# Linear attention and a token/channel mixer: where the hand-over sums and the last products stand around the last batch

## The chip, the cores and the metric

The kernel runs on one core of a Trainium2 chip. The metric is device time in microseconds, lower is better. Engines are named as the profile names them: PE (TensorE matmul), PEld (its weight loads), DVE (VectorE), ACT (ScalarE), POOL (GpSimd), SP (SyncE, used for transfers).

## What is computed

Linear attention with elu+1 features over batch 8, 8 heads, 576 tokens, 64 columns a head; its output, with heads side by side (512 columns), goes through a mixer over tokens (576 to 256 and back) and one over channels (512 to 1536 and back), each with a residual sum.

```
def phi(x): return np.where(x > 0, x, np.exp(x) - 1.0) + 1.0
q_p, k_p = phi(q), phi(k)
kv  = einsum('bhsd,bhse->bhde', k_p, v);  z = k_p.sum(axis=2)
x   = einsum('bhsd,bhde->bhse', q_p, kv) / (einsum('bhsd,bhd->bhs', q_p, z) + 1e-6)
xt  = x.transpose(0, 2, 1)
u   = x + (relu(xt @ w_tok1) @ w_tok2).transpose(0, 2, 1)
out = u + relu(u @ w_ch1) @ w_ch2
```

## The kernel before

The batches run one after another. The 576 tokens of a batch are four full row tiles of 128 and a tail of 64; the tails of two batches share one tile. PE computes in bf16 into eight PSUM banks, each named by hand.

The channel mixer of a batch is `mm3` (u @ w_ch1, twelve slices `mc`, each evicted with relu by ACT or DVE into `cr`) and then its second product. For most batches the second product is in Strassen-Winograd form: seven half-size products (`pair_product`, L779, six matmuls each, for j = 0 and 1) instead of eight. `ORDER` is 1, 2, 6, 5, 7, 3, 4. Their operands need differences of blocks (`row_sums` on DVE, weight differences on DVE and POOL), and their results three PSUM tiles, X, Z and Y. `pair_end` (L788) adds u to a tile on DVE and, where a term is shared, a copy of it on POOL (L790). `pair_put` (L794) writes a batch out from POOL's queue.

For the batches 2 to 6 a loop builds a list `big` of PE's large steps (12 of `mm3`, then the 14 pair products) and a list `fill` of everything else, with the step that it follows: `put(b0 + 12, u_sums, which)` places an operation after big step 24. All engines take their instructions in the order in which this emits them. `b0` is 12 for batch 6, so steps b0 to b0 + 13 are its pair products. The next batch's attention and token mixer are among the fill, and its u reaches `uT` by DMA transposes (`utr_dma`, L512).

The last batch, 7, is emitted by `last_block` from a written string, `SEQUENCE`. Its letters are:

- `m` g i: `mix_first(g, i)`, product i of the *first* channel product, also in Winograd form, for slice group g (L703, four matmuls). It needs the weight differences of `first_sums` and the u differences of `u_sums` (L680, four DVE instructions that read `uT`). Results i = 1, 5 and 6 are copied by ACT (L712), 4 is evicted with relu by ACT (L710), 2, 3 and 7 are added to a held copy by DVE (L715) and pass a relu later (L686).
- `c` i: `mm3_tails(i)`, the tails of the last four batches (L557), relu by ACT (L559), in bank 2 or 3.
- `r` k: the four `row_sums` for two of six hidden slices (L653, DVE).
- `p` i j: `product(n, j, i)`, second channel product i for the row tile pair j (L733, six matmuls). Each is followed by a DVE sum into `obuf` (L739). Pair 0 is written out once, after p40 (L762); pair 1 in four parts, after p21, p71, p31 and p41 (L759). A half goes from SP's queue and a half from ACT's.
- `q` e third: `tail_third`, a third of the tails' second product (L579, four matmuls of 512 columns); after the last third a DVE sum (L583) and the output (L585).

A product that adds to a PSUM tile has to wait until the sum of the earlier product has read that tile: p60, p70 and p40 share one tile with p10, p30 follows p50, p20 stands alone; the same for pair 1. m02 and m12 both use bank 0. Batch 6's tile X lies in bank 2, tile Y in bank 3, tile Z in bank 0; c0 uses bank 2. Batch 1's `mm3` has its own list of banks, by mc.

Of the kernel before, what the change touches and what calls it, by code (L numbers as in the profile page):

```python
# [18 lines left out]
def kernel(  # L19
# [45 lines left out]
    def bank(at=None):  # L65
        if at is None:
            at, ring[1] = ring[1], (ring[1] + 1) % 4
        return psum[:, at]
# [453 lines left out]
    def mm3(n, mc, kjs=range(NDM), dve=False):  # L522
        b = n % 2
        if kjs[0] == 0:
            part_of[mc] = bank(None if n == 0 else (
                (0, 1, 0, 1, 2, 3, 0, 1, 2, 3, 0, 1) if n > 1 else
                (3, 5, 7, 0, 3, 1, 2, 0, 3, 1, 0, 1))[mc])
        ps = part_of[mc]
        for kj in kjs:
            nc.tensor.matmul(out=ps, lhsT=wc1[:, kj, 128 * mc:128 * mc + 128],  # L530
                             rhs=uTj[b][:, kj] if n < 2 else uT[b][:, :, kj],
                             start=(kj == 0), stop=(kj == NDM - 1))
        if kjs[-1] == NDM - 1 and dve:
            nc.vector.tensor_scalar(out=cr[b][:, mc, :], in0=ps, scalar1=0.0, scalar2=None,
                                    op0=ALU.max)
        elif kjs[-1] == NDM - 1:
            nc.scalar.activation(out=cr[b][:, mc, :], in_=ps, func=AF.Relu)  # L537
# [117 lines left out]
    def row_sums(n, which, k0, m):  # L655
        winograd(sb, [ablock(n, i, e) for e in range(2) for i in range(2)], which,
                 slice(k0, k0 + m))
# [10 lines left out]
    def cblock(m, h):  # L668
        return wc1[:, 2 * h:2 * h + 2, HM * m:HM * (m + 1)]

    def ublock(h, e):
        return uT[1][:, 2 * e:2 * e + 2, 2 * h:2 * h + 2]
# [11 lines left out]
    def mix_relu():  # L684
        o = mixed.pop(0)
        nc.vector.tensor_scalar(out=o, in0=o, scalar1=0.0, scalar2=None, op0=ALU.max)  # L686
# [6 lines left out]
    def mix_first(g, i):  # L693
        ps = bank({1: (1, 4, 7), 6: (1, 4, 7), 7: (1, 4, 7), 4: (1, 4, 7), 2: (0, 0, 0),
                   5: (5, 6, 5), 3: (5, 6, 5)}[i][g]).rearrange("p (j c) -> p j c", j=2)
        first = i in (1, 2, 5)
        lhs, rhs = {1: (cblock(0, 0), ublock(0, 0)), 2: (cblock(0, 1), ublock(1, 0)),
                    3: (sw[3], ublock(1, 1)), 4: (cblock(1, 1), tu[3]), 5: (sw[0], tu[0]),
                    6: (sw[1], tu[1]), 7: (sw[2], tu[2])}[i]
        for j in range(2):  # L700
            cs = slice(128 * (2 * g + j), 128 * (2 * g + j) + 128)
            for k_ in range(2):
                nc.tensor.matmul(out=ps[:, j], lhsT=lhs[:, k_, cs], rhs=rhs[:, :, k_],  # L703
                                 start=(first and j == 0 and k_ == 0), stop=(k_ == 1),
                                 skip_group_check=not first or j == 1)
        c1, c6, c5 = hold[g]
        held_back = len(mixed)
        dst = lambda m, e: cr[1][:, KH * m + 2 * g:KH * m + 2 * g + 2, HALF[e]]
        if i == 4:
            nc.scalar.activation(out=dst(1, 0), in_=ps, func=AF.Relu)  # L710
        elif i in (1, 6, 5):
            nc.scalar.copy(out={1: c1, 6: c6, 5: c5}[i], in_=ps)  # L712
        else:
            o, c = {2: (dst(0, 0), c1), 3: (dst(0, 1), c6), 7: (dst(1, 1), c5)}[i]
            nc.vector.tensor_tensor(out=o, in0=ps, in1=c, op=ALU.add)  # L715
            mixed.append(o)
        if held_back:
            mix_relu()
# [67 lines left out]
    def pair_end(n, tile_, d, c, i=None):  # L786
        o = live["o4"][:, d::2, HC[c]]
        nc.vector.tensor_tensor(out=o, in0=live[tile_], in1=u[n % 2][:, d::2, HC[c]], op=ALU.add)  # L788
        if i is not None:
            nc.gpsimd.tensor_tensor(out=o, in0=o, in1=part[i], op=ALU.add)  # L790

    def pair_put(n):
        for e in range(2):
            nc.gpsimd.dma_start(out=outv[n, :, e:e + 7:2], in_=live["o4"][half[e]])  # L794
# [2 lines left out]


    SEQUENCE = """m01 m02 m11 m05 m15 m06 m12 c0 m21 m03 m16 m07 c1 m25 m13 m22 m17 m04 c2 m26 m14
        m23 c3 m27 r0 c4 m24 r2 c5 q00 q01 p10 r4 p20 q02 p11 q10 p60  # L800
        p50 q11 p21 p70 q12 p30 p61 p40 p51 p71 p31 p41"""

    def last_block(n):
        for e in SEQUENCE.split():
            a = [int(c) for c in e[1:]]
            if e[0] == "m":
                mix_first(*a)
            elif e[0] == "c":
                mm3_tails(*a)
            elif e[0] == "p":  # L810
                product(n, a[1], a[0])
            elif e[0] == "q":
                tail_third(*a)
            else:
                while mixed:
                    mix_relu()
                for which in range(1, 5):
                    row_sums(n, which, a[0], 2)

    def m4s(n):  # L820
        return [lambda i=i, j=j: pair_product(n, i, j) for i in ORDER for j in range(2)]
# [117 lines left out]
    for mc in range(2):  # L939
        mm3(0, mc, range(0, 2))  # L940
# [88 lines left out]
    put = lambda s, fn, *a: fill.append((s, lambda: fn(*a)))  # L1029
# [53 lines left out]
    for n in range(2, B - 1):  # L1083
        p, b = divmod(n, 2)
        tail = int(n == 3)
        big = m3(n) + m3t * tail + m4s(n) + m4(p, [8]) * tail
        b0 = 12 + 3 * tail
        todo = dict(steps(n + 1))
        fill = []
        put = lambda s, fn, *a: fill.append((s, lambda: fn(*a)))  # L1090
        at = lambda s, *nms: [put(s, todo.pop(nm)) for nm in nms if nm in todo]

        def phi_at(nm, ex, ad, en):
            for g in range(2):
                if ex is not None:
                    put(ex[g], phi_exp, nm, n + 2, 2 * g, 2)
            for g in range(2):
                put(ad[g], phi_add, nm, n + 2, 2 * g, 2)
                put(en[g], phi_end, nm, n + 2, 2 * g, 2)

        at(1, "nd")
        if n + 2 < B:
            if n > 3:
                phi_at("k", None, (2, 2), (3, 4))
                put(5, load_all, n + 3, "k")
            if n != 3:
                phi_at("q", (7, 7), (8, 9), (9, 10))
            else:
                phi_at("k", (7, 7), (8, 9), (9, 10))
            put(10, *((qtr_dma, n + 2) if n != 3 else (load_all, n + 3, "k")))  # L1110
            if n == 2:
                for g in range(2):
                    put(10, phi_add, "k", n + 2, 2 * g, 2)
        at(7, "mm1")
        for s, k0 in ((11, 0), (12, 3)):
            for w in (1, 2):
                put(s, row_sums, n, w, k0, 3)
        if n == 3:
            phi_at("q", (12, 13), (13, 13), (14, 14))
            put(15, qtr_dma, n + 2)  # L1120
        at(13, "mm2a", "uta")
        put(14, row_sums, n, 3, 0, KH)
        put(b0 + 1, pair_copy, 0)
        if n == 2:
            for g in range(2):
                put(b0 + 1, phi_exp, "k", n + 2, 2 * g, 2)
                put(b0 + 2, phi_end, "k", n + 2, 2 * g, 2)
            put(b0 + 4, load_all, n + 3, "k")
        at(b0 + 3 - tail, "mm2b", "utb")
        put(b0 + 4 - tail, row_sums, n, 4, 0, KH)  # L1130
        put(b0 + 4 - tail, pair_end, n, "Z", 0, 0, 0)
        put(b0 + 5, pair_copy, 1)
        if n + 2 < B:
            for g in range(2):
                put(b0 + (5 if n == 2 else 2) + g, vcast, n + 2, g)
        put(b0 + 7, load_all, n + 3, "qv")
        put(b0 + 7, pair_copy, 2)
        if n > 2 and n + 3 < B:
            put(b0 + 8, k_exp, n + 3)
        put(b0 + 9, pair_end, n, "X", 1, 1, 2)  # L1140
        if n == B - 2:
            at(b0 + 6, "mm2t", "utt")
        at(b0 + 9, "mm2t")
        if n + 2 < B:
            put(b0 + 9, kv, n + 2, range(2))
        at(b0 + 9, "utt")
        put(b0 + 11, pair_end, n, "Y", 0, 1, 1)
        if n == B - 2:
            for which in range(1, 5):
                put(6, first_sums, which)  # L1150
                put(b0 + 12, u_sums, which)
        put(b0 + 13, pair_end, n, "X", 1, 0)
        put(b0 + 13, pair_put, n)
        assert not todo, todo
        run(big, sorted(fill, key=lambda e: e[0]))

# [30 lines left out]
```

## Time and profile before

| | |
|---|---|
| median of 6 runs | 251.55 us |
| the runs | 251.1, 251.88, 251.19, 253.54, 256.08, 251.21 us |
| profiled execution | 251.1 us, span 249.3 us |
| busy | PE 241.1, DVE 184.8, ACT 140.2, POOL 67.3 us |
| granted TensorE clock | 1.00 |

A profile gives one execution. Its span runs from the first to the last instruction; the time contains 1.8 us more around it. Times inside it are microseconds from the span's start. In a group's line the columns are line, engine, operation, what is written from what, count, busy time and mean; in a chain each row has start, length and what ran; in a timeline the same, with the engine's idle time before it in brackets.

### The profile page before, as it was taken

To read this page: it belongs to the slowest core of one execution; us is meant where nothing else is said; L and a number is where in the kernel's file an instruction comes from. 1 tells how busy PE (TensorE), PEld (TensorE's weight loads), DVE (VectorE), ACT (ScalarE), POOL (GpSimd) and SP (SyncE) were. 2 spreads that over 40 slices of the span, in tenths; PEclk is the share of its full clock that TensorE was granted. 3 is DMA by queue.
4 is the path that set the end of the run, shared out by engine and by line. 5 is a ranking of instruction groups with operands and counts; after the bars stand their busy time and mean duration, and the time that the engine had idled before them with its cause. 6 is when DMAs were issued, how large, how long until landed. Compare 5 with 4: busy or idle time off the path is not lost.

```text
span 249.3 us, 5904 instructions
## 1 busy us (share of the span) xinstructions
PE 241.1 (97%) x2418; PEld 155.1 (62%) x2418; DVE 184.8 (74%) x327; ACT 140.2 (56%) x224; POOL 67.3 (27%) x78
## 2 busy tenths in 40 slices
PE   7999999999999999999999999999999999999992
PEld 3584455554767545774688446774587457888672
DVE  5954778899998369956793497759874959767852
ACT  4764791578774378736886278647843661356000
POOL 9760030496703500070004400260016001420000
PEclk9999999999999999999999999999999999999999
DMA  6999999999639996599939956697261705170035
GB/s 250 266 203 257 364 244 322 342 283 292 236 52 253 241 399 91 99 313 377 268 83 215 387 160 199 121 380 177 59 121 22 151 0 85 23 158 14 0 97 158
DMA packets 49771, 48.39 MB, mean 194 GB/s; under 512 B 30032, under 2 KB 35536, under 8 KB 49744
## 3 DMA queue, kind: packets, MB, share of 16 engines
q1 hardware_dynamic: 41648, 35.00, 48.4%
q0 software_dynamic: 7472, 12.22, 22.4%
q10 hardware_dynamic: 624, 0.79, 1.0%
q8 instruction: 19, 0.31, 0.5%
q14 instruction: 8, 0.07, 0.1%
HBM read 35.85 MB, written 9.44 MB: 182 GB/s over the span
## 4 chain that ended last, share of the span: by engine, by line
PE 92%; DVE 3%; DMA 2%; ACT 1%; issue 1%; DVEq 0%
PE ps L530 30%; PE ps L779 22%; PE ps L570 6%; PE ps L303 6%; PE ps L316 4%; PE ps L733 4%; PE ps L703 3%; PE ps L544 2%; PE ps L557 2%; PE ps L579 2%; PE ps L189 2%; PE ps L259 2%; DMA k_raw<-in_k_dram 2%; PE ps L200 1%; PE ps L465 1%; DVE q_raw L680 1%
## 5 line engine op out<-in xcount | busy, mean ns | idle before, releaser
L530 PE MATMUL ps<-uT,wc 128*128 128x512 bf16 x336 | 76.4, 379 | 0.0
L537 ACT ACTIVATE cr<-ps 128x512 bf16<-128x512 f32 x79 | 46.0, 600 | 34.0 <-PE ps L530 33.5
L530 PEld LDWEIGHTS <-wc 128*128 128x128 bf16 x336 | 32.0, 98 | 37.5 <-issue 1.0
L790 POOL TENSOR_TENSOR obuf<-obuf,q_raw 128x512 f32<-128x512 f32 x6 | 7.6, 1268 | 94.2 <-ACT w L784 74.5
L788 DVE TENSOR_TENSOR obuf<-ps,u 128x512 f32<-128x512 f32 x24 | 16.3, 687 | 12.5 <-PE ps L779 9.4
L779 PE MATMUL ps<-k_raw,v_raw 128*128 128x256 bf16 x216 | 24.9, 273 | 0.0
L779 PEld LDWEIGHTS <-cr 128*128 128x128 bf16 x216 | 21.0, 98 | 4.6
L779 PEld LDWEIGHTS <-v_raw 128*128 128x128 bf16 x216 | 21.0, 98 | 3.9 <-issue 0.4
L149 ACT ACTIVATE e<-q_raw 128x1152 bf16<-128x1152 f32 x16 | 18.3, 1160 | 6.4 <-DVE den L241 5.2
L149 ACT ACTIVATE e<-k_raw 128x1152 bf16<-128x1152 f32 x16 | 18.2, 1163 | 3.6 <-DMA k_raw<-in_k_dram 3.6
L653 DVE TENSOR_TENSOR v_raw<-cr 128x768 bf16<-128x768 bf16 (+2 forms) x24 | 14.8, 618 | 5.0 <-ACT cr L537 5.0
L272 DVE TENSOR_TENSOR x<-ps,dens 128x768 bf16<-128x768 f32 x18 | 17.2, 958 | 0.6
L779 PE MATMUL ps<-wc,cr 128*128 128x256 bf16 x144 | 17.7, 273 | 0.0
L328 DVE TENSOR_TENSOR u<-ps,x 128x1024 bf16<-128x1024 f32 x12 | 14.7, 1221 | 1.8 <-PE ps L316 1.5
L163 DVE TENSOR_TENSOR kp<-e,y 128x1152 bf16<-128x1152 bf16 x16 | 11.8, 751 | 3.5 <-ACT e L149 3.4
L303 PE MATMUL ps<-x,w 128*128 128x512 bf16 x56 | 14.4, 379 | 0.0
L163 DVE TENSOR_TENSOR qp<-e,y 128x1152 bf16<-128x1152 bf16 x16 | 11.9, 756 | 3.3 <-ACT e L149 2.5
L155 DVE TENSOR_SCALAR y<-q_raw 128x1152 bf16<-128x1152 f32 x16 | 13.7, 867 | 0.0
L174 ACT CAST vs<-v_raw 128x1152 bf16<-128x1152 f32 x12 | 13.5, 1164 | 0.0
L155 DVE TENSOR_SCALAR y<-k_raw 128x1152 bf16<-128x1152 f32 x16 | 11.8, 763 | 2.3 <-DMA k_raw<-in_k_dram 2.3
L316 PE MATMUL ps<-ar,w2p 128*128 128x512 bf16 x50 | 12.9, 379 | 0.0
L790 POOL TENSOR_TENSOR obuf<-obuf,part 128x512 f32<-128x512 f32 x6 | 7.6, 1267 | 16.0 <-DVE obuf L788 16.0
(160 smaller groups left out, 392.1 us busy)
## 6 DMA issues: line engine op xcount, KB each, us to landing
k_raw<-in_k_dram SPq DMA_DIRECT2D x16, 576.0 KB, 6.4
q_raw<-in_q_dram SPq DMA_DIRECT2D x16, 576.0 KB, 6.1
v_raw<-in_v_dram SPq DMA_DIRECT2D x14, 576.0 KB, 10.3
out_dram<-obuf POOLq DMA_DIRECT2D x12, 512.0 KB, 6.5
wc<-in_moe_w_ch_dram POOLq DMA_DIRECT2D x8, 384.0 KB, 10.1
out_dram<-obuf POOLq DMA_DIRECT2D x4, 256.0 KB, 5.5
cr<-in_v_dram POOLq DMA_DIRECT2D x2, 288.0 KB, 7.0
out_dram<-obuf POOLq DMA_DIRECT2D x4, 128.0 KB, 7.8
```

What stands on the lines that cost most here:

```text
L149: nc.scalar.activation(out=e, in_=f, func=AF.Exp)
L155: nc.vector.tensor_scalar(out=y, in0=f, scalar1=1.0, scalar2=1.0, op0=ALU.add, op1=ALU.max)
L163: live["phi"] = nc.vector.tensor_tensor(out=dst.transpose([0, 2, 1, 3]), in0=e.rearrange("p (i t d) -> p i t d", i=nj, t=T), in1=y.rearran ...
L272: nc.vector.tensor_tensor(out=xv[:, :, rc0:rc0 + 3], in0=v_[:, :, k0:k0 + 6, 0:D].rearrange("p i (q a) d -> p i q a d", a=2), in1=den[:, : ...
L303: nc.tensor.matmul(out=ps[:, mt], lhsT=w1t[:, b, ms] if r == R else w1[:, r, ms], rhs=x[b][:, r, :], start=(r == 0), stop=(r == R))
L316: nc.tensor.matmul(out=ps[:, i], lhsT=w2v(kt, r, b), rhs=ar[b][:, kt, :], start=(kt == 0), stop=(kt == NT - 1 and not add))
L530: nc.tensor.matmul(out=ps, lhsT=wc1[:, kj, 128 * mc:128 * mc + 128], rhs=uTj[b][:, kj] if n < 2 else uT[b][:, :, kj], start=(kj == 0), sto ...
L537: nc.scalar.activation(out=cr[b][:, mc, :], in_=ps, func=AF.Relu)
L570: nc.tensor.matmul(out=ps, lhsT=crt[:, kc, :] if t == 8 else cr[b][:, kc, 128 * r:128 * r + 128], rhs=wc2[:, kc, :], start=(kc == 0), stop ...
L779: nc.tensor.matmul(out=live[tile_][:, j], lhsT=lhs[:, k_], rhs=rhs[:, k_], start=(first and j == 0 and k_ == 0), stop=(k_ == KH - 1), skip ...
L788: nc.vector.tensor_tensor(out=o, in0=live[tile_], in1=u[n % 2][:, d::2, HC[c]], op=ALU.add)
L790: nc.gpsimd.tensor_tensor(out=o, in0=o, in1=part[i], op=ALU.add)
```

## The change

Four edits:

- Batch 1's `mm3` puts mc 7 into bank 7 instead of bank 0.
- In batch 6's block the four sums of u are emitted after step b0 + 10 (product 3 of j = 0) instead of b0 + 12 (product 4 of j = 0). They come ahead of the end sum of Y (b0 + 11).
- The last end sum of batch 6's tile X and its output are no longer emitted after the block's last step, but in the last block, after m02.
- `SEQUENCE` is the same up to q00; behind it the same products, thirds and row sums have another order.

```diff
-                (3, 5, 7, 0, 3, 1, 2, 0, 3, 1, 0, 1))[mc])
+                (3, 5, 7, 0, 3, 1, 2, 7, 3, 1, 0, 1))[mc])
...
-        m23 c3 m27 r0 c4 m24 r2 c5 q00 q01 p10 r4 p20 q02 p11 q10 p60
-        p50 q11 p21 p70 q12 p30 p61 p40 p51 p71 p31 p41"""
+        m23 c3 m27 r0 c4 m24 r2 c5 q00 p10 r4 q01 p20 q02 p60 q10 p50
+        q11 p70 q12 p11 p30 p21 p40 p61 p51 p71 p31 p41"""
...
                 mix_first(*a)
+                if e == "m02":
+                    pair_end(n - 1, "X", 1, 0)
+                    pair_put(n - 1)
...
                 put(6, first_sums, which)
-                put(b0 + 12, u_sums, which)
-        put(b0 + 13, pair_end, n, "X", 1, 0)
-        put(b0 + 13, pair_put, n)
+                put(b0 + 10, u_sums, which)
+        else:
+            put(b0 + 13, pair_end, n, "X", 1, 0)
+            put(b0 + 13, pair_put, n)
```

## The prediction

> **What bounds the kernel now.** I read the page's busy rows first, then who waits for whom on PE, then the chain that ended last around the last block, then the SP queue at the end.
>
> ```profile
> PE 241.1 (97%) x2418; PEld 155.1 (62%) x2418; DVE 184.8 (74%) x327; ACT 140.2 (56%) x224; POOL 67.3 (27%) x78
> ## 2 busy tenths in 40 slices
> PE   7999999999999999999999999999999999999992
> ...
> PEclk9999999999999999999999999999999999999999
> ```
>
> PE is full in all but the first and last slice, at full granted clock. So TensorE's products bound the kernel; what can go is the few places where PE stands still, and the end after its last product. The change touches neither the start nor the number of products. The waits of PE, longest first, name three places, of which the change touches the second and, as will be seen, the third:
>
> ```profile
> PE ps L843 <- DVE ones L856: 1.5, 1, 1.5
> PE ps L703 <- DVE cr L715: 0.6, 1, 0.6
> PE ps L544 <- DVE x L279: 0.4, 1, 0.4
> ```
>
> The chain of waits around the second one, where batch 6's block hands over to the last block:
>
> ```profile
> 214.04 0.06 DVE obuf L788
> 214.10 0.55 issue
> 214.65 0.45 DVE q_raw L680
> 215.10 0.02 issue
> 215.12 1.44 DVE q_raw L680 x2
> 216.56 0.19 issue
> 216.75 0.41 DVE q_raw L680
> 217.16 0.60 DVE obuf L788
> 217.77 0.61 DVE cr L715
> 218.38 0.04 issue
> 218.42 0.60 PE ps L703 x4
> ```
>
> VectorE works through the end sum of tile Y (L788 at 214.04), the four sums of u (L680), the last end sum of tile X (L788 at 217.09), and only then adds m02 (L715), which empties PSUM bank 0. Product m12 goes into bank 0, so PE waits. The view calls it 0.6 us with modelled ends. By pace it is more: the timeline has 12 matmuls of L703 from 216.36, chained groups of 12 such take 1.31 us, so m12 was due at 217.67 and started at 218.42: **0.75 us**.
>
> The end: the last DVE sum is 244.85 to 245.27, the span 249.3. Between lie the last outputs.
>
> ```profile
> 242.66 0.65 SPq L762 DMA_DIRECT2D out_dram<-obuf  x1
> 243.97 2.54 SPq L759 DMA_DIRECT2D out_dram<-obuf  x3
> ```
>
> Taken in short windows, the three of L759 (p71, p31, p41; 64 KB each on SP and again on ACT) are issued at 243.97 for 0.48 us, 244.64 for 1.23 us, and 245.96 for 0.55 us on SP and 0.79 on ACT. The data of p41 was there at 245.27, yet its issue began 0.69 us later, because p31's took 1.23 us. Ahead of them stands p40's output (L762, 256 KB on each queue, issued at 242.66), which landed 3.2 us (SP) and 4.2 us (ACT) later. p41 lands 2.3 us after its issue on ACT, at 248.3; the last 1.0 us of the span is the closing barrier.
>
> **The change, part by part.**
>
> **1. Sums of u and the end sum of X.** The instruction order on DVE becomes: end sum X of the earlier column half (212.70 to 213.39), the four sums of u, end sum Y, m02's add, end sum X, m02's relu. Nothing is added; two orders change. Step by step, in before's times:
> - u sum 1 starts when the end sum of X is over, about 213.3 (instructions in this queue overlap by 0.08 us), and takes 0.44. It reads the transposed u of the last block. Of the two transposes the first was issued at 207.1 and landed 4.6 us later, the second at 209.2 and landed 3.2 us later: 212.4, so 0.9 us early.
> - GpSimd's add for that X (L790, 213.54, 1.26 us) now overlaps the sums. In the trace one L680 beside an L790 took 1.37 us instead of 0.41: it ended 0.28 after the L790 did. I take the same again: L790 starts 213.54, stretched to 1.40 as its neighbour was, ends 214.94; u sum 2 ends about 215.2, u sums 3 and 4 at 215.6 and 215.9.
> - End sum Y 215.8 to 216.5, m02's add 216.4 to 217.1. It needs ScalarE's copy of m01, which ended at 216.27, so that isn't late.
> - m12 finds bank 0 free at 217.1, 0.57 before it is due. **The whole 0.75 us goes.**
> - What is late next: end sum X ends at 217.7 and frees bank 2 for c0, due after m12 at 217.67 + 0.44 = 218.11. It is 0.4 early. The relu of m02 may be held by GpSimd's second add (starts 216.65, 1.26 us) until 218.2; the next DVE work, m12's add, comes at 218.3. ScalarE's copy of m21 writes the buffer which that add reads; it was at 220.44 and comes to 219.7, against 217.9.
> - pair_put on POOL needs both end sum X (217.7) and the second L790 (217.9): 218.0 to 218.3, as now, and nobody waits for its landing before p11's obuf slots, 20 us later.
>
> The Trainium skill, "SBUF — State Buffer", section "Who interferes with whom", says that a VectorE instruction with two SBUF inputs and a GpSimd instruction that reads SBUF exclude each other for the whole instruction, and whoever issues first wins. Row: one L680 of the four was held, by 0.96 us. Rule at its worst, GpSimd first at u sum 1 too: that sum ends at 215.1 instead of 213.74, the rest follows freely, m02's add ends about 217.5 and end sum X about 218.1. m12 still starts on time and c0 loses about 0.05. I take the row; the two differ by 0.05 us of the end. Bounds of this part: 0 (one more sum held for 1.26 us) to 0.75.
>
> **2. mm3 of batch 1, mc 7 from bank 0 to bank 7.** mc 7 now waits for ScalarE's relu of mc 3: the matmul at 57.81 is 0.15 late against its neighbours' pace, and it starts 0.05 after that relu ended at 57.76. Bank 7's last user, mc 2, is long gone, so this 0.15 goes. But the next thing PE meets is the third wait above: the tail product at 64.6 waits for nd_all's first quotient (L279). DVE is busy without a break from 57.6 to 65.1 (phi's pass L155 alone 60.84 to 63.59, beside GpSimd's weight sums), and none of that waits for mc 7. PE comes 0.15 earlier and waits 0.15 longer. **I take 0**; bounds 0 to 0.15. nd_all's third bank pair contains bank 7, but mc 7's relu ended at 60.3 and nd_all starts at 62.2.
>
> **3. The last products, re-ordered.** The same products and thirds, 0.655 us each product (six at 0.109) and 0.865 each third. p40 ends five products before the end instead of four.
> - p10 and r4: q01 moves behind r4, p10's add comes when DVE is free at 232.2, r4's four row sums end at 234.1 instead of 234.8. p60, which reads the second of them (ready at 233.4), moves from 235.69 to 234.18: 0.8 us of cover. If it were gone, PE would wait by the difference.
> - p71 now follows p61 with only p51 between. p71 adds to the tile that p61's add must have read. p31 after p51, and p41 after p71, stand like that already, and start 0.03 late each. **Loss 0.03.**
> - The outputs, per queue in order: q02 at 235.1, q12 at 239.65, p21 at 241.35, p40 at 242.0 (was 242.66), then p71, p31, p41 as they were. The 512 KB of p40 leave 0.65 earlier, and so does whatever held p31's issue. It then takes 0.55 to 0.6, p41 is issued with its data at 245.33 instead of 245.96, and at the same 2.3 us to landing the end comes **0.63 earlier**. p21's 128 KB now stand 0.65 ahead of p40, and 4 KB per engine and queue are soon out of its way.
>
> Here a rule speaks against costing more, or less. "Perfetto Trace Analysis", DMA Instruction — HWDGE, says that the issue in a profile contains a wait for the descriptor generator, which one queue at a time holds. By that, p31's 1.23 against 0.48 is such a wait and goes as p40 moves. "DMA: Bandwidth & Descriptors", Anatomy of one DMA, puts about 2.0 us fixed beside the bytes' time, for GpSimd's path. By this alone p41 would land 2.1 to 2.2 us after 245.33 and the end gains 0.75 to 0.85. The rows (2.1 on SP, 2.3 on ACT, with p71 and p31 landing 3.1 us after theirs) show a backlog as well, and I stay with 0.63. p21's output, with only an instruction fetch beside it, landed 2.9 us (SP) and 3.1 us (ACT) after issue; at 3.1 p41 would land at 248.4, 0.1 later than now. Bounds -0.1 to 0.85.
>
> **Sum.** -0.75 + 0 + 0.03 - 0.63 = -1.35 us. Profiled execution 251.1 us (span 249.3): 249.75, span about 248.0. Three of six runs lie at 251.10 to 251.21; the median, 251.55, is lifted by 253.54 and 256.08. I forecast **249.8 us**, 0.7% under the median. About 1% (2.5 us) is what a measurement of this kernel can tell from no change.
>
> **Rivals.**
> - *The stall moves from m12 to c0* (0.12). End sum X stands behind m02's add now. If GpSimd's adds hold the sums once more (1.26 us), m02's add ends at 218.4 and end sum X at 219.0; PE is held as before or a little longer. For: the held L680. Against: only one L790 can run there, since the next needs end sum Y, behind the sums. Only part 3 remains: 251.1 - 0.6 = 250.5.
> - *The end is a backlog* (0.15). p21's output right before p40's delays it by as much as it was moved. For: both queues share the engines, three outputs of 128 KB follow each other every 0.66 us, and p21's alone took as long as p71's behind it. Against: p40's own issue has 0.65 less in front of p31. Only part 1 remains: 250.4.
> - *Slower: the sums of u meet the transposes* (0.05). In the queue of DVE u sum 1 now stands ahead of end sum Y, m02's add and end sum X. If the second transpose lands late, all of them wait. Landings of L512 range from 3.0 to 6.1 us. At 6.1 (215.3) m12 starts as late as now, and part 3's gain is left: 250.5. From 216.0 on, 6.8 us after issue, the kernel is slower than before, one for one; at 8 us after issue 252.3. Against: 3.2 us here, with nothing else on the queues then.
> - *More goes than I count* (0.06): the end gains 0.85 and part 2 its 0.15: 249.3.
> - Forecast 0.56; undone by something that I don't see, about 251.5: 0.06.
>
> Both lesser rivals lie within 1%, as the forecast does. Faster by over 1% means under 249.0, only the edge of the fourth; slower by over 1% needs the third at its far end or runs disturbed as two of six were. The range takes in the parts' bounds, 249.35 and 251.2, with 0.2 us on either side for runs that differ.
>
> **What would show it.** PE's wait L703 <- L715 gone; one L680 still at 1.4 us, the first starting near 213.3; PE's wait L544 <- L279 grown from 0.4 to 0.5; L762 0.65 us earlier against PE's end, p31's issue near 0.55 us, and SP's three last issues 1.9 us in sum instead of 2.54. Wrong if L703 waits at c0's bank or L557 waits for L788, or if p31's issue still takes 1.2 us.

## The result, and the profile after

| | before | after |
|---|---|---|
| runs | 72 | 35 |
| lowest | 250.94 us | 249.79 us |
| lower quartile | 251.34 us | 250.04 us |
| median | 251.63 us | 250.79 us |
| upper quartile | 252.68 us | 251.91 us |
| profiled execution (span) | 251.1 us (249.3) | 252.05 us (250.3) |

The ratio of after to before is 0.9965, with an interval of 0.9949 to 0.998: a gain of 0.35%, 0.84 us between the medians. Runs over 1.5% above the fastest of their kernel (7 of before, 1 of after) are in this table and this paragraph, but are left out of the quartiles, medians, ranges and counts of the experiments. The forecast was 249.8 us, 0.7% under the median. At the lower quartile the gain is 1.30 us, close to the forecast sum of 1.35; at the median half of a microsecond of it is missing. And the one profiled execution of after is *longer* than that of before. The profile shows where this comes from. First the busy row, and PE's slices and granted clock, of the page of after:

```profile
PE 240.0 (96%) x2418; PEld 154.8 (62%) x2418; DVE 184.7 (74%) x327; ACT 140.4 (56%) x224; POOL 67.4 (27%) x78
...
PE   7799999999999699999999999999999999999994
...
PEclk9999999999999999999999999999999999999999
```

The number of matmuls is the same and the clock is full, but slice 14 of PE, which was a 9, is a 6: PE stands still in a place that the change does not touch. The waits of PE in after name it:

```profile
PE ps L530 <- DMA uT<-u: 2.0, 1, 2.0
PE ps L846 <- DVE ones L859: 1.5, 1, 1.5
PE ps L200 <- DVE qp L163: 1.2, 1, 1.2
PE ps L544 <- DVE x L279: 0.5, 1, 0.5
```

Two things are to be seen. The wait that the change aimed at, L703 <- L715, is gone. A wait of 2.0 us that before did not have heads the list: `mm3` of batch 2 (L530) waits for the transposed u of batch 2 (L512). The chain that ended last in after, around that place:

```profile
79.47 1.13 DVE u L328
80.59 0.03 DVE obuf L788
80.62 5.27 DMA uT<-u
85.90 0.05 issue
85.94 1.90 PE ps L530 x8
```

The second transpose of batch 2's u, issued at 80.62, takes 5.27 us to land. In before the same one took 3.2 us. So I cut each trace into three stretches: the start to the first pair product of batch 1 (L779), from there to the first `mm3` matmul of batch 2 (L530), and from the last block's first matmul (m01, L703) to the end of the span.

| | first pair product | to batch 2's `mm3` | m01 | m01 to the end |
|---|---|---|---|---|
| before | 66.98 | 16.54 | 215.05 | 34.27 |
| after | 67.37 | 18.57 | 217.47 | 32.79 |

(Columns one and three are points in time, two and four lengths, in us.) From the first `mm3` matmul of batch 2 to m01 it is 131.53 us in both: nothing differs there. The change's own stretch, the last, is **1.48 us shorter**; the stretch with the transpose is 2.03 us longer, and the start 0.39 us.

The hand-over, from DVE's timeline in after (start, length, what; idle time before it in brackets):

```profile
215.12 0.69 DVE L788 TENSOR_TENSOR obuf<-ps,u 128x512 f32<-128x512 f32 x1 [0.67 <-PE ps L779]
215.73 0.41 DVE L680 TENSOR_TENSOR q_raw<-uT 128x512 bf16<-128x512 bf16 x1
216.18 1.37 DVE L680 TENSOR_TENSOR q_raw<-uT,q_raw 128x512 bf16<-128x512 bf16 x1
217.47 0.41 DVE L680 TENSOR_TENSOR q_raw<-uT 128x512 bf16<-128x512 bf16 x1
217.81 0.41 DVE L680 TENSOR_TENSOR q_raw<-uT,q_raw 128x512 bf16<-128x512 bf16 x1
218.15 0.68 DVE L788 TENSOR_TENSOR obuf<-ps,u 128x512 f32<-128x512 f32 x1
218.75 0.68 DVE L715 TENSOR_TENSOR cr<-ps,v_raw 128x512 bf16<-128x512 f32 x1
```

The order is the new one, with all sums of u done 0.5 us before m02's add. Against m01 (217.47 here, 215.05 before) the add starts 1.28 us after it instead of 2.64. One L680 in four still takes 1.37 us, held beside GpSimd's add, and it costs nothing. The chain shows PE running through the hand-over in one piece, and, in its last row, the last sum:

```profile
212.95 4.69 PE ps L779 x42
217.64 3.06 PE ps L703 x28
220.69 0.87 PE ps L557 x8
...
246.61 0.42 DVE obuf L739
```

The end, from SP's timeline:

```profile
243.06 0.47 SPq L759 DMA_DIRECT2D out_dram<-obuf  x1
243.68 0.65 SPq L762 DMA_DIRECT2D out_dram<-obuf  x1
245.77 2.05 SPq L759 DMA_DIRECT2D out_dram<-obuf  x3
```

p40's output is issued 2.9 us before PE's last product ends instead of 2.2. From the start of SP's first of the three last issues to the end of the last it is 2.05 us instead of 2.54; the one of p31 among them takes 0.73 us on SP and 0.50 on ACT instead of 1.23 and 1.15. From the end of the last DVE sum (247.03) to the end of the span it is 3.24 us instead of 4.05.

### The profile page after: what moved, and what is told of

Read it like the earlier page. It is cut to its first block, busy times and chain, and to the rows that moved or that the text cites. A ratio compares the mean times of both kernels' runs of the same rounds, so it can differ in the third digit from the quotient of the medians.

```text
span 250.3 us, 5907 instructions
## 1 busy us (share of the span) xinstructions
PE 240.0 (96%) x2418; PEld 154.8 (62%) x2418; DVE 184.7 (74%) x327; ACT 140.4 (56%) x224; POOL 67.4 (27%) x78
## 4 chain that ended last, share of the span: by engine, by line
PE 74%; DMA 13%; DVE 5%; POOL 3%; issue 2%; ACT 1%; SPq 0%; POOLq 0%; DVEq 0%
PE ps L530 21%; PE ps L779 21%; DMA wc<-in_moe_w_ch_dram 6%; PE ps L303 6%; DMA q_raw<-in_q_dram 5%; PE ps L570 4%; PE ps L316 4%; PE ps L733 4%; PE ps L703 4%; DMA uT<-u 2%; PE ps L557 2%; PE ps L579 2%; PE ps L544 2%; PE ps L259 1%; PE ps L189 1%
## 5 line engine op out<-in xcount | busy, mean ns | idle before, releaser
L530 PE MATMUL ps<-uT,wc 128*128 128x512 bf16 x336 | 76.2, 379 | 2.0 <-DMA uT<-u 2.0
L530 PEld LDWEIGHTS <-wc 128*128 128x128 bf16 x336 | 32.0, 98 | 39.4 <-DMA uT<-u 2.4
L788 DVE TENSOR_TENSOR obuf<-ps,u 128x512 f32<-128x512 f32 x24 | 16.3, 687 | 11.8 <-PE ps L779 8.8
L779 PE MATMUL ps<-k_raw,v_raw 128*128 128x256 bf16 x216 | 24.9, 273 | 0.0
L779 PEld LDWEIGHTS <-cr 128*128 128x128 bf16 x216 | 21.1, 98 | 4.5
L779 PEld LDWEIGHTS <-v_raw 128*128 128x128 bf16 x216 | 21.1, 98 | 3.9 <-issue 0.4
L779 PE MATMUL ps<-wc,cr 128*128 128x256 bf16 x144 | 17.7, 273 | 0.0
L570 PE MATMUL ps<-wc,cr 128*128 128x512 bf16 x48 | 12.0, 379 | 0.3 <-DMA wc<-in_moe_w_ch_dram 0.3
## 6 DMA issues: line engine op xcount, KB each, us to landing
wc<-in_moe_w_ch_dram POOLq DMA_DIRECT2D x8, 384.0 KB, 10.1
```

Source lines behind the costliest of these rows:

```text
L570: nc.tensor.matmul(out=ps, lhsT=crt[:, kc, :] if t == 8 else cr[b][:, kc, 128 * r:128 * r + 128], rhs=wc2[:, kc, :], start=(kc == 0), stop ...
L779: nc.tensor.matmul(out=live[tile_][:, j], lhsT=lhs[:, k_], rhs=rhs[:, k_], start=(first and j == 0 and k_ == 0), stop=(k_ == KH - 1), skip ...
```

## The experiments

Stretches below are those of the second table. Each ratio is to runs of before on the same chip, with its 95% interval.

### First question: do the parts do what their sum says?

Theory: the parts work as forecast, and the missing half microsecond is the late transpose, which is not theirs. Rivals: a part is worth less than forecast, or the bank edit in batch 1, the only one ahead of the transpose, makes it late.

**e1_handover**, before with the hand-over's edits alone:

```diff
+                if e == "m02":
+                    pair_end(n - 1, "X", 1, 0)
+                    pair_put(n - 1)
...
-                put(b0 + 12, u_sums, which)
-        put(b0 + 13, pair_end, n, "X", 1, 0)
-        put(b0 + 13, pair_put, n)
+                put(b0 + 10, u_sums, which)
+        else:
+            put(b0 + 13, pair_end, n, "X", 1, 0)
+            put(b0 + 13, pair_put, n)
```

> Before, with the hand-over edits alone (sums of u at b0 + 10, end sum of X and its output after m02). Theory A (the parts are worth what the sum says, the shortfall is executions in which something early in the kernel comes late, in either kernel alike): stretch from m01's first matmul to the span's end 0.75 us shorter than 34.27 us of before, so 33.5; time 0.7 us under before in the lower quartile of runs, ratio about 0.997. Theory B (the bank edit makes batch 2's transposes late): the same here, and no PE wait on uT of some 2 us. Theory C (the hand-over's gain is taken back at c0 or in the end): stretch 34.0 to 34.3, ratio 1.000.

**e2_sequence**, before with the new order of the last products alone:

```diff
-        m23 c3 m27 r0 c4 m24 r2 c5 q00 q01 p10 r4 p20 q02 p11 q10 p60
-        p50 q11 p21 p70 q12 p30 p61 p40 p51 p71 p31 p41"""
+        m23 c3 m27 r0 c4 m24 r2 c5 q00 p10 r4 q01 p20 q02 p60 q10 p50
+        q11 p70 q12 p11 p30 p21 p40 p61 p51 p71 p31 p41"""
```

> Before, with the new SEQUENCE alone. Theory A: m12's wait stays (0.75 by pace), stretch from m01 to the span's end 33.5 to 33.6 (0.63 to 0.8 shorter), time 0.6 to 0.7 us under before in the lower quartile, ratio about 0.9975. Theory B: the same, no 2 us wait on uT. Theory C: stretch 34.2 or more.

**e3_bank**, before with the bank edit alone:

```diff
-                (3, 5, 7, 0, 3, 1, 2, 0, 3, 1, 0, 1))[mc])
+                (3, 5, 7, 0, 3, 1, 2, 7, 3, 1, 0, 1))[mc])
```

> Before, with mc 7 of batch 1 in bank 7 alone. Theory A: 0 within 0.2 us; the 0.15 us before mc 7 goes, the wait for L279 is 0.5 instead of 0.37, and waits of PE on uT come as often as in before. Theory B: slower than before by 0.3 to 0.5 us in the median, the profile or the upper half of the runs shows a wait of PE on uT of 1 to 2 us. Theory C: 0.

**e4_no_bank**, after without the bank edit:

```diff
-                (3, 5, 7, 0, 3, 1, 2, 7, 3, 1, 0, 1))[mc])
+                (3, 5, 7, 0, 3, 1, 2, 0, 3, 1, 0, 1))[mc])
```

> The changed kernel without its bank edit (mc 7 back in bank 0). Theory A: as the changed kernel, lower quartile 1.25 us under before, stretch from m01 to the end 32.8, upper half of the runs 1 to 2 us above the lower as in both kernels. Theory B: its median is also 1.2 to 1.3 us under before, ratio 0.995, 0.4 us better than the changed kernel. Theory C: as the changed kernel.

Measured, with before's quartiles on that chip 251.44, 251.74 and 252.99:

| | m01 to the end | PE's wait for L512 in the profile | lower quartile, median | ratio |
|---|---|---|---|---|
| e1_handover | 33.56 (-0.71) | 0.4 | 250.76, 251.05 | 0.9979 (0.9954 to 1.0005) |
| e2_sequence | 33.59 (-0.68) | 1.9 | 250.57, 251.01 | 0.9978 (0.9953 to 1.0003) |
| e3_bank | 34.26 (-0.01) | 2.4 | 251.56, 252.06 | 1.0023 (0.9997 to 1.0048) |
| e4_no_bank | 32.97 (-1.30) | 0.7 | 250.05, 250.18 | 0.9925 (0.9903 to 0.9947) |

In the stretch of the change the two large parts give 0.71 and 0.68 us, and 1.30 together without the bank edit. The bank edit gives nothing. The gains at the lower quartiles (0.68, 0.87, -0.12 and 1.39) and at the medians (0.69, 0.73, -0.32 and 1.56) are of about these sizes, but of the four ratios only that of e4_no_bank has an interval clear of 1: the sizes of the parts rest on the stretches, one profile each. The waits of PE in e2_sequence and e3_bank:

```profile
PE ps L530 <- DMA uT<-u: 1.9, 1, 1.9
PE ps L200 <- DVE qp L163: 1.6, 1, 1.6
PE ps L843 <- DVE ones L856: 1.5, 1, 1.5
PE ps L703 <- DVE cr L715: 0.6, 1, 0.6
```

```profile
PE ps L530 <- DMA uT<-u: 2.4, 1, 2.4
...
PE ps L703 <- DVE cr L715: 0.6, 1, 0.6
PE ps L544 <- DVE x L279: 0.5, 1, 0.5
```

The late transpose is there in e2_sequence, which has none of the edits ahead of it. So it isn't the change that makes it, or not the change alone. The times say the same of before: 20 of its 65 runs lie more than 0.9 us above the tenth percentile (I call such runs late); of after 16 of 34. A difference of that size or more arises by chance one time in eight (Fisher's test). Not every late run is late in this place: the profiled execution of e1_handover, 252.31 us, waited 0.4 us for the transpose, but its first pair product started at 68.46 us, where the other thirteen traces have 66.74 to 67.61.

### Second question: is the spread of before and of after that transpose?

Between the second transpose of qT (L219) and the first of uT, SP's queue issues the two q loads of batch 4 (L130, 576 KB each). SP's timeline in before, then in after:

```profile
71.54 3.12 SPq L219 DMA_TRANSPOSE qT<-qp  x2
74.75 1.35 SPq L130 DMA_DIRECT2D q_raw<-in_q_dram  x2
76.20 5.27 SPq L512 DMA_TRANSPOSE uT<-u  x2
```

```profile
71.92 3.56 SPq L219 DMA_TRANSPOSE qT<-qp  x2
75.58 1.38 SPq L130 DMA_DIRECT2D q_raw<-in_q_dram  x2
77.05 4.97 SPq L512 DMA_TRANSPOSE uT<-u  x2
```

The loads were issued 7.8 and 8.7 us after the first pair product in before, 8.2 and 9.1 after it in after, since the two L219 in front took 3.56 us to issue instead of 3.12. Theory: these loads are what the second transpose of u lands behind. Issued after it, they leave its landing near 3 us in every execution; both kernels then have the same narrow spread, and their medians differ by the whole sum. Rival: the transpose is late by itself, or the next loads take their place.

**f1_before_qlate** and **f2_after_qlate**, the same edit to each of the two kernels, which moves the q loads behind the second transpose:

```diff
-    put(16, load_all, 4, "q")
+    put(25, load_all, 4, "q")
     put(25, load_all, 4, "kv")
```

> Before, with the loads of q for batch 4 issued after batch 2's u transposes instead of ahead of them. Theory A (the upper part of both kernels' runs is PE's wait for those transposes, whose landing varies between 3.2 and 5.8 us beside the q loads): both transposes land within 3.5 us of issue, no PE wait on uT, the runs lie together near the lower quartile of before (251.2 to 251.5), median 0.3 to 0.5 us under before, few runs over 252. Theory B (only the bank edit makes them late): no difference from before. Rival E (the spread has another cause, the start or the last block): spread as before.

> The changed kernel, bank edit and all, with the same move of the q loads. Theory A: runs together at 249.8 to 250.2, median 1.3 us under the same edit of before, 1.6 us or more under before, ratio 0.993. Theory B (the bank edit costs by itself): 0.3 to 0.5 us slower than that, ratio 0.995. Rival E: spread and median as the changed kernel, ratio 0.9965.

**f3_before_qclose**, before with the q loads between the two transposes, to make the second one late:

```diff
+    put(24, load_all, 4, "q")
     put(24, todo["utb"])
-    put(16, load_all, 4, "q")
```

> Before, with the q loads issued between batch 2's last u sum and its second u transpose, so that they always run beside it: the suspected collision made certain. Theory A: PE waits 1.5 to 3 us for uT in the profile, median 253 or more, the low runs of 251.2 are gone. Rivals B and E: as before within 0.3 us.

| | second L512, issue to landing | PE's wait for it | median (range) | ratio |
|---|---|---|---|---|
| f1_before_qlate | 3.1 | 0 | 251.05 (250.75 to 251.6), 22 runs | 0.9968 (0.9949 to 0.9987) |
| f2_after_qlate | 3.1 | 0 | 249.68 (249.3 to 250.18), 15 runs | 0.9907 (0.9879 to 0.9934) |
| f3_before_qclose | 4.1 | 0.8 | 251.77 (251.16 to 253.07), 12 runs | 0.9989 (0.9958 to 1.0019) |

The answers on DMA issues, each cut to a few tenths of a microsecond around the issue of that transpose (the last number is from issue to landing), are of before, of after, and of f2_after_qlate:

```profile
uT<-u SPq DMA_TRANSPOSE x1, 3.2
```

```profile
uT<-u SPq DMA_TRANSPOSE x1, 5.3
```

```profile
uT<-u SPq DMA_TRANSPOSE x1, 3.1
```

And the waits of PE in f2_after_qlate have neither L530 nor L703:

```profile
PE ps L200 <- DVE qp L163: 1.8, 1, 1.8
PE ps L846 <- DVE ones L859: 1.5, 1, 1.5
PE ps L544 <- DVE x L279: 0.5, 1, 0.5
PE ps L494 <- DVE u L477: 0.3, 1, 0.3
```

With the loads out of the way none of 37 runs is late, where before had 14 of 40 beside them. Before's range there, 250.87 to 254.57, shrinks to 250.75 to 251.6. The granted clock is no rival for these: it was 0.995 or more in 13 of the 14 late runs. So nearly the whole spread of both kernels hangs on where those q loads stand. The profiles show what it goes through: the loads are issued after the first pair product, and from batch 2's first `mm3` matmul to m01 all fourteen traces have 131.51 to 131.53 us, so that only the stretch between can tell where the loads stand. It goes from 16.46 us (f1, f2) to 19.06 (e3), and what PE waits for in it is the second transpose. And the two medians differ by **1.37 us: the forecast sum, once both kernels are measured undisturbed.** f2_after_qlate is faster than before and, by the ratios to before (0.9907 and 0.9965), than after.

f3_before_qclose was a miss of mine. I had expected the transpose to be late in nearly every run. SP went straight on after the first transpose, so that the loads were issued at 10.1 and 10.7 us and had landed at 14.8 and 16.2; the transpose, issued at 13.26, took 4.1 us, less than in after. The wait was 0.8 us, and the median that of before.

### Third question: which instruction carries each part?

**g1_swap**, before with p40 one product earlier and nothing else:

```diff
-        p50 q11 p21 p70 q12 p30 p61 p40 p51 p71 p31 p41"""
+        p50 q11 p21 p70 q12 p30 p40 p61 p51 p71 p31 p41"""
```

> Before, with p40 and p61 exchanged in SEQUENCE and nothing else: p40's output starts one product (0.65 us) earlier. If the end's gain comes from that alone: p31's issue takes 0.5 to 0.8 us instead of 1.23, the stretch from m01's first matmul to the span's end is 33.5 to 33.7 instead of 34.27, as with the whole new SEQUENCE (33.59). If it comes from the other moves (q01, p11 and p21 later, p10 and r4 earlier): 34.1 to 34.3.

**g2_x_moved**, before with the end sum of X behind m02's add, the sums of u left where they were:

```diff
+                if e == "m02":
+                    pair_end(n - 1, "X", 1, 0)
+                    pair_put(n - 1)
...
-        put(b0 + 13, pair_end, n, "X", 1, 0)
-        put(b0 + 13, pair_put, n)
+        if n < B - 2:
+            put(b0 + 13, pair_end, n, "X", 1, 0)
+            put(b0 + 13, pair_put, n)
```

> Before, with batch 6's last end sum of X and its output moved behind m02, the sums of u left where they were. On DVE: end sum Y, four sums of u (one of them held beside GpSimd), m02's add, end sum X. If the two edits of the hand-over simply add, m02's add ends at 217.7 in before's times, 0.6 us earlier than 218.36, and m12 starts 0.1 us late at most: stretch from m01 to the end 33.6 to 33.7 (before 34.27, both edits 33.56). If the sums' place is what matters: 34.0 or more.

**g3_sums_moved**, before with the other half, the sums of u moved and X left where it was:

```diff
-                put(b0 + 12, u_sums, which)
+                put(b0 + 10, u_sums, which)
```

> Before, with the sums of u two steps earlier, the end sum of X left ahead of m02's add. On DVE: sums of u, end sum Y, end sum X, m02's add: the same work ahead of m02's add as in before, begun 1.3 us earlier. If the order of end sum X is what matters: m02's add is as late as now, stretch 34.1 to 34.3. If the earlier start is enough: m02's add ends at 217.7 to 217.8, m12 0.1 us late, stretch 33.6 to 33.7.

One time and one profile each: g1_swap 250.41 us, stretch 33.63 (-0.64); g2_x_moved 251.46 us, 33.85 (-0.42); g3_sums_moved 250.91 us, 33.55 (-0.72).

The swap of two products gives nearly all of what the whole new sequence gives (0.64 of 0.68); p31's issue took 0.47 us on SP and 0.74 on ACT. Of the hand-over, moving the sums gives everything, and the move of X adds nothing to it; alone, X gave 0.42, between the two values that I had set against each other. DVE's timeline of g3_sums_moved, where both sums of L788 still stand ahead of m02's add:

```profile
215.92 0.41 DVE L680 TENSOR_TENSOR q_raw<-uT,q_raw 128x512 bf16<-128x512 bf16 x1
216.25 1.27 DVE L788 TENSOR_TENSOR obuf<-ps,u 128x512 f32<-128x512 f32 x2
217.45 0.68 DVE L715 TENSOR_TENSOR cr<-ps,v_raw 128x512 bf16<-128x512 f32 x1
```

The add ends at 218.13, 2.55 us after m01's start (215.58); m12 is due 2.62 us after it. It is in time by 0.07 us. The move of X turns this into 0.7 us of slack and no time. In g2_x_moved, on PE's timeline, m12 (the row of four) and c0 (L557) start late, by pace 0.15 and 0.16 us:

```profile
217.15 1.47 PE L703 MATMUL ps<-q_raw,k_raw 128*128 128x256 bf16 x12
218.61 0.60 PE L703 MATMUL ps<-uT,wc 128*128 128x256 bf16 x4
219.20 1.03 PE L557 MATMUL ps<-uTt,wc 128*128 128x256 bf16 x8
```

That is the forecast's first rival, the stall that passes to c0, though only where the sums of u still stand in front of the moved X.

### Fourth question: what stays of the bank edit, and is there more at the end?

**f4_no_bank_qlate**, f2_after_qlate with mc 7 back in bank 0:

```diff
-                (3, 5, 7, 0, 3, 1, 2, 7, 3, 1, 0, 1))[mc])
+                (3, 5, 7, 0, 3, 1, 2, 0, 3, 1, 0, 1))[mc])
```

> The changed kernel without its bank edit and with the q loads of batch 4 late: it prices the bank edit where no transpose is late. Forecast's step (the 0.15 us is swallowed by the wait for L279): 249.68 us median within 0.1, as with the edit. If the bank edit is worth 0.15: 249.8. If it costs by itself: 249.3 or less.

**h1_p40_earlier**, p40 ahead of p21 as well:

```diff
-        q11 p70 q12 p11 p30 p21 p40 p61 p51 p71 p31 p41"""
+        q11 p70 q12 p11 p30 p40 p21 p61 p51 p71 p31 p41"""
```

> The changed kernel with the q loads of batch 4 late and p40 ahead of p21, so its output leaves another 0.65 us earlier: a version to beat both. If p40's output still holds the last three: p31's issue on SP takes 0.48 instead of 0.73 us, p41 is issued on SP 0.15 to 0.2 us earlier, stretch from m01 to the end 32.65, median 249.5. If the end has come down to the landing of p41 alone: 249.6 to 249.7, the same.

f4_no_bank_qlate: 249.56 us (249.34 to 250.2, 6 runs), ratio 0.9903 (0.9874 to 0.9933), stretch 32.84. h1_p40_earlier: 249.67 us (249.6 to 250.02, 6 runs), 0.991 (0.9883 to 0.9937), stretch 32.97. Both are the 249.68 and 32.83 of f2_after_qlate within what they can tell. With no transpose in the way the bank edit is worth nothing, and p40's output has no more to give by an earlier place. On SP the three last issues take 0.47 us each in h1, but on ACT p31's still takes 0.70, and p41's begins 0.4 us after its data is there; it lands last, 2.4 us after the data, where in f2 the last landing comes 2.3 us after it.

## Why the forecast was right in its parts and too large in its total

- **The hand-over, 0.75 forecast.** Measured 0.71 (e1) and 0.72 (g3); up to PE's last product it is 0.75 in both. Right, including the held L680 at 1.37 us: the Trainium skill's rule in "SBUF — State Buffer", "Who interferes with whom", was weighed at its worst, two sums held, and the row of one in four was the better guide. The trace agrees with the rule itself, that whoever issues first goes first: in after the first sum started at 215.73, ahead of GpSimd's add at 215.96, and took 0.41 us; the second was held until 0.28 us after that add. The sums, not X, carry the gain. "What is late next" was named correctly as c0: in after the end sum of X ends 0.5 us before c0 starts, 0.4 forecast.
- **The bank edit, 0 forecast.** Right. The wait L544 <- L279 takes up what mc 7 gives, as forecast: 0.4 became 0.5 in after and e3.
- **The order of products, 0.03 lost.** Measured 0.09: ahead of p71 PE stands still for 93 ns in after, e2 and f2. In g1, with the same p61 p51 p71, it is 24 ns; what makes the difference was not tested.
- **The end, 0.63 forecast.** Measured 0.81 in after and 0.77 in e2, from the last sum to the end of the span. p31's issue did lose most of its wait, though not all: 0.73 us on SP, not 0.55, so that p41's on SP began 0.2 us after its data was there. But the landings behind it were 2.1 us on SP and 1.9 on ACT, where ACT's had been 2.3, and the last one came 2.3 us after the data instead of 3.0. The forecast stayed with the row, which left 0.1 to 0.2 us to the other reading (the Trainium skill, "DMA: Bandwidth & Descriptors", "Anatomy of one DMA", about 2.0 us fixed, for GpSimd's path); the landings measured are close to that figure. The backlog rival fell: p40's output landed 3.2 us (SP) and 3.9 us (ACT) after issue with p21's right ahead of it, against 3.2 and 4.2.
- **The sum, 1.35 forecast.** 1.48 in the stretch of after, 1.37 between the medians of f1 and f2. The difference of 0.13 is mostly the end's 0.18 more, less the 0.06 more that the order of products lost.
- **The step that failed: from the profiled execution to the median.** The prediction's words are "Three of six runs lie at 251.10 to 251.21; the median, 251.55, is lifted by 253.54 and 256.08", and then it sets 249.8 us. The sum was made on an execution without the late transpose, and its result set as the median, as if after would have no such runs. That took 1.75 us off a median from which 1.35 was to go. The lift is not a stray of two runs: 20 of before's 65 runs and 16 of after's 34 are late, and f1 and f2 show that the q loads ahead of the transpose make them so. 251.55 - 1.35 = 250.2 us would have been the consistent forecast; with after's larger share of late runs, which chance alone may account for, 250.79 came out. When nearly half of the runs are late, the median falls between the two groups and depends on that share: drawing the runs of the first table anew at random gives a gain between the medians of 0.0 to 1.5 us in 95 of 100 draws, which holds 1.35 as well as 0.84.

It could have been seen. In before's trace the transpose lands 16.50 us after the first pair product and `mm3` starts at 16.54. In f1, where the loads are away, it lands at 16.32 and `mm3` starts at 16.46, when PE reaches it. So in the "undisturbed" profile that I read PE was *already* waiting for this landing, by less than 0.1 us: a wait of no length in the list, and no slack at all. The view of L512 in before, from which the forecast took its "3.0 to 6.1 us", names one waiter in the whole kernel, a weight load of `mm3` (PEld):

```profile
who waited for it (us, times):
  PEld L530: 0.4, 1
```

The forecast left that row out. It is 0.2 in f1 and f2, where the transpose lands in time, and 2.4 in after. The prediction looked at the landings of L512, 3.0 to 6.1 us, but asked only what a late one would do at the hand-over, where the slack was 0.9 us. At batch 2 it was zero, and 2 us more of landing is 2 us more of time.

What stays open: why the two L219 take 3.0 us to issue in one execution and 4.1 in another, which puts the q loads nearer to the transpose; how a load ahead of it makes the transpose land late; what made the start of e1's profiled execution long; and whether the bank edit makes late executions more frequent (late runs with it: e3 9 of 18, after 16 of 34; without it: e4 3 of 18, before 20 of 65 and, on e3's chip, 21 of 63: too few to tell).

## What to carry to other kernels

A sum made on one profiled execution is a difference: add it to the level of executions of the same kind, and find what makes the others longer before giving a median. When runs of one kernel spread by per cents, look for a transfer that lands just as its reader comes; PE's list of waits shows it as nothing, while its landing set beside the reader's start shows that there is no slack, and the view of the transfer's own line shows who waits. And of a change of several edits, look for the one row that carries each gain: here a swap of two products (0.64 us) and one moved row of sums (0.72 us) measured by themselves come to 1.36 of the 1.48, while two loads moved behind a transpose took another 0.6 us off before's median (f1) and 1.1 off after's (f2, on another chip).

## What the runs showed of the hardware that I had not expected

- The second transpose of u landed 3.1 us after its issue where no load had been issued since the first one (f1, f2), and mostly later the nearer the two 576 KB loads stood: 3.1 us with the first of them issued 7.7 us after the first pair product (g1), 3.2 at 7.8 (before), 3.6 at 7.9 (g3), 5.3 at 8.2 (after and e2), 5.8 at 8.4 (e3). The transpose itself was always issued at 13.26. It is no strict rule: g2 had 4.1 at 7.9, e1 3.7 at 8.1, e4 4.0 at 8.7, and f3 4.1 at 10.1.
- What shifts those loads is the issue of the two transposes (L219) ahead of them, 3.12 us in before and 3.56 in after and in e2, though in after no edit lies in front of them but a PSUM bank, and in e2 none.
- A small output behind a large one paid in its *issue*: on SP 1.23 us for p31's 64 KB with p40's output issued 2.0 us before (before), 0.73 with it 2.75 us before (after), 0.47 with it 3.4 us before (h1). The output issued just ahead of it, p71's, took 0.47 or 0.48 in all three, so being close behind is not what costs. In the seven traces with before's order of products the long issue ended within 0.03 us of the landing of p40's half on SP; whether it waits for that landing was not tested.
